# Pooled q and k in four buffers each, v of batch 0 pooled by two additions, the exponent table loaded at the start, no forced filler matmuls, and a new order for every engine

## The chip, the core and the metric

The kernel runs on one core of a Trainium2 chip, as one program on its engines: TensorE (PE in the rows; PEld is its weight load), VectorE (DVE), ScalarE (ACT), GpSimd (POOL) and SyncE (SP, which only issues transfers here). The metric is the device time of one launch in microseconds; lower is better.

## The reference

Three stages in a chain. The inputs of the last two are set so that every product of the matrices is wanted at nearly float32 precision, which the kernel reaches by splitting each operand into a high and a low float32r part and adding three matmuls.

```python
# attention: B, H, S, D = 4, 8, 576, 64; pooled by 4 along S, plus a local band of +-3
q_d, k_d, v_d = (mean over groups of 4 positions of q, k, v)      # 144 positions
out_d     = softmax(q_d k_d^T / sqrt(D)) v_d
out_local = softmax(q k^T / sqrt(D), only |i - j| < 4) v
x = (repeat(out_d, 4) + out_local) as (2304, 512)
# first stage: 2304 x 512 -> 2048 -> 512
h = relu(x w_in); x = (s * h * h + b) w_out
# second stage: 2304 x 512 -> 1536 -> 512
return ((x w_a) * (x w_b)) w_out
```

## The kernel before, in words

**Stages.** The first stage of the MLP runs in 6 blocks of 384 positions; each block is 16 iterations of 12 matmuls into `h` and 12 into four `acc` banks (`a_iter`, L1044), 24 matmuls of 384 columns per iteration, 2304 in all. Its input for block i, `xsh` and `xsl`, comes from the attention. The second stage (`b_group`, matmuls at L1347 and L1487 to L1489) follows when the last block is done.

**Attention on two engines.** Batch 0 and the first 192 positions of batch 1 are done as 8 *tiles* of 96 positions on TensorE (`tile_job`): scores, maximum (DVE), exponents (ACT), division (DVE), transposes (PE), copies (ACT), product with v (PE), sum with the pooled part (DVE), split into `xsh` (ACT) and `xsl` (DVE). Most later positions are done as 13 *units* on VectorE (`unit`, "the band" below): products `pr`, sums, exponents, products with v, three additions of which the last, at L984, writes the unit's output `o`; then four transposes on PE, `bt` at L999, put it in the layout that the first stage needs. The pooled attention of a batch and a pair of heads is `down`: sums over four positions (`kd`, `qd` from DVE for batch 0, from POOL for the others), scores, maximum `nb`, exponents, transposes, copies, product with pooled v. For batches 1 to 3 the pooled v, `pv`, is summed by accumulating transfers that POOL issues (`pool_in`, L551); for batch 0 DVE sums it by a reduction over a strided view (L603).

**Weights.** The weights come as 64-bit words. Each of the 32 slices of the first stage needs three ACT instructions (L342, L349, L378) and three DVE instructions (L354, L362, L383) before PE can use it. The exponents of the tiles, the copies and these slices all stand in ACT's one queue. The stretch from the start until the last slice is done is called the ramp here. When the ramp's work is over, its buffers are given to the band (`open_b`), so the first `pr` of the band comes after the last slice.

**What sets the order.** `Program` collects tasks with an engine, a planned duration, what they read and the buffers they take; `Program.order` simulates the engines with the planned durations and writes each engine's instructions in the order in which its simulation starts them. Each engine then runs its own list strictly in that order. A few instructions are put in by the function of another engine's task and have no duration in the plan: the two casts of the mask and of the identity on DVE (`i_fn`, `m_fn`, L293 to L301), which stand in DVE's list wherever the plan happens to issue the two transfers on SP. PE's idle time ahead of the first `h` is filled with matmuls on zeros (`keep_warm`, `pw` at L273): 18 at the start, then in front of each PE task at least `FILL_MIN` of them.

Of the kernel before, what the change touches and what calls it, by code (L numbers as in the profile page):

```python
# [55 lines left out]
MAX_STAGED = 4  # L56

# [52 lines left out]
class Program:  # L110
# [26 lines left out]
    def order(self):  # L137
# [9 lines left out]
        clock, warming = Clock(), True  # L147
# [10 lines left out]
        while len(out) < len(self.tasks):  # L158
# [47 lines left out]
            at[t.eng] = t.end  # L206
            avail[t.eng].remove(t)
# [26 lines left out]
def moe_chain(ctx, tc, qT, kT, vd, tq, tk, tv, qu, ku, vu, w_a1, w_o1, w_a2, w_b2, w_o2, sb, ident_d, bmask_d, emask_d, out):  # L234
# [19 lines left out]
    ones = const.tile([128, 2], F32, name="ones")  # L254
    bc = const.tile([128, HP], F32, name="bc")
# [283 lines left out]
    def pool_in(b, after, due):  # L539
# [3 lines left out]
        for r in range(4):  # L543
            for kh in range(2):
                def fn(p, r=r, kh=kh):
# [8 lines left out]
                    "POOL" if r else "SP", 1.25, fn, (), [("pv", b)] if r == 3 else (), () if r + kh else [("pv",)], (), due,  # L554
                    [t[kh]] if r else [t[0]] if kh else after, seen=6.0,
                )

    def down(b, hp, ph, pool_eng, v_eng, due=1e9):
# [16 lines left out]
        for name, src in (("k", "dk"), ("q", "dq")):  # L575
            eng = pool_eng[name == "q"]

            def prep(p, name=name, eng=eng):
# [9 lines left out]
                eng, dve(S) if eng == "DVE" else 1.25, prep, [(src, key)], [(name + "d", key)],  # L588
                [(ph + name + "d",)], [ph + (dq if src == "dq" else src)] if b else (),
            )  # L590
        if b == 0:
            for kh in range(2):
                def lv(p, kh=kh):
                    st["v", kh] = new(ph, "dv", [HK, 4, 2 * D])
                    return st["v", kh], vd[b, hp, :, kh]

                load(lv, HK * 2048, writes=[("dv", key, kh)], acq=[(ph + "dv",)], after=after)

                def vprep(p, kh=kh):
                    x = st["v", kh]  # L600
                    d = st["vp", kh] = new(ph, "vp", [HK, 2 * D])
                    if v_eng == "DVE":
                        V.tensor_reduce(out=d, in_=x.rearrange("p r c -> p c r"), axis=AX.X, op=ALU.add)  # L603
                    else:
                        G.tensor_tensor(out=x[:, 0:2], in0=x[:, 0:2], in1=x[:, 2:4], op=ALU.add)
                        G.tensor_tensor(out=d, in0=x[:, 0], in1=x[:, 1], op=ALU.add)

                add(
                    v_eng, dve(512) if v_eng == "DVE" else 1.1, vprep, [("dv", key, kh)], [("vp", key, kh)],
                    [(ph + "vp",)], [ph + "dv"],  # L610
                )
# [75 lines left out]
        def o_fn(p):  # L687
# [9 lines left out]
            "PE", 0.6, o_fn, [("aT", key), ("upslot", b)] + ([("vp", key, 0), ("vp", key, 1)] if b == 0 else [("pv", b)]),  # L697
            [("o", key)], [wide], [pick(ts, 2)] + ([ph + "vp", ph + "vp"] if b == 0 else ["pv"] if hp == HP - 1 else []),
# [992 lines left out]
```

## Time and profile before

| | |
|---|---|
| device time, median of 3 runs | 936.18 us (935.21 to 938.07) |
| span of the profiled execution, first to last instruction | 932.3 us |
| so outside the span, against the three runs | 2.9 to 5.8 us, 3.9 at the median |
| PE busy | 913.2 us, 98% of the span |
| DVE busy | 789.9 us, 85% |
| ACT busy | 497.4 us, 53% |
| POOL busy | 69.7 us, 7% |
| mean granted TensorE clock | 0.994 of full speed |

The profile gives the span of its execution and no device time of that execution; sums below are made on the span and then moved by the 3.9 us to the median. The shares are means over stages that differ: ACT is busy nearly all the time in the first 140 us and little afterwards.

### The profile page before, as it was taken

What the parts mean: (1) busy time and instruction counts of PE and PEld (TensorE: products, weight loads), DVE (VectorE), ACT (ScalarE), POOL (GpSimd) and SP (SyncE); (2) the same over time, 40 slices, a digit from 0 to 9 for tenths busy, and PEclk for the clock granted to TensorE, in tenths of its full rate; (3) what the DMA queues carried; (4) which work ended last, traced back from release to release, by engine and by line L of the source; (5) the groups of instructions that cost most, each with busy time, mean ns of one, the idle gap of its engine ahead of it and who ended that gap; (6) DMA issues with size and microseconds to landing.
All of it is one profiled execution on the core that took longest, in us unless ns stands there. A gap on an engine that the chain in (4) does not pass through costs nothing.

```text
span 932.3 us, 14367 instructions
## 1 busy us (share of the span) xinstructions
PE 913.2 (98%) x5319; PEld 847.0 (91%) x5319; DVE 789.9 (85%) x1388; ACT 497.4 (53%) x1144; POOL 69.7 (7%) x70
## 2 busy tenths in 40 slices
PE   8988999999999999999999999999999999999997
PEld 4667989998999899999999999999999999999996
DVE  6988998999999999995977999879877778877753
ACT  4989995345445443535988555335433336433322
POOL 2241201021322200000000000000000000000000
PEclk9998999999999999999999999999999999999999
DMA  7869626224354332313477342012200010300001
GB/s 206 241 174 332 156 90 194 82 82 133 115 115 114 103 107 69 102 29 136 148 262 261 122 122 82 23 44 81 102 22 3 24 43 13 102 29 18 1 1 69
DMA packets 46864, 96.76 MB, mean 104 GB/s; under 512 B 6393, under 2 KB 21337, under 8 KB 46409
## 3 DMA queue, kind: packets, MB, share of 16 engines
q1 hardware_dynamic: 39160, 92.77, 31.0%
q0 software_dynamic: 7200, 2.67, 2.5%
q8 instruction: 42, 0.69, 0.3%
q10 hardware_dynamic: 432, 0.39, 0.1%
q14 instruction: 30, 0.24, 0.1%
HBM read 83.22 MB, written 12.58 MB: 103 GB/s over the span
## 4 chain that ended last, share of the span: by engine, by line
PE 84%; DVE 5%; ACT 4%; issue 3%; DMA 2%; POOL 1%; SPq 0%; ACTq 0%
PE ab L1347 28%; PE acc L1102 7%; PE acc L1103 6%; PE h L1059 6%; PE acc L1104 6%; PE h L1061 6%; PE h L1060 6%; PE acc L1488 5%; PE acc L1489 5%; PE acc L1487 5%; DVE pr L969 1%; DMA pv<-in_vd_dram 1%; ACT z L342 1%; DMA tq<-in_bmask_dram 1%; ACT w L378 1%
## 5 line engine op out<-in xcount | busy, mean ns | idle before, releaser
L1347 PE MATMUL ab<-xo,w 128*128 128x384 f32 x1376 | 273.7, 338 | 0.4 <-DVE u L1390 0.4
L1347 PEld LDWEIGHTS ab<-xo,w 128*128 128x128 f32 x1376 | 246.1, 188 | 16.3 <-DVE u L1390 0.7
L1102 PE MATMUL acc<-gh,w 128*128 128x384 f32 (+1 forms) x384 | 134.2, 350 | 4.0 <-ACT w L816 2.0
L1103 PE MATMUL acc<-gl,w 128*128 128x384 f32 x384 | 131.2, 342 | 0.0
L1059 PE MATMUL h<-xsh,w 128*128 128x384 f32 x384 | 131.1, 341 | 0.0
L1104 PE MATMUL acc<-gh,w 128*128 128x384 f32 (+1 forms) x384 | 130.5, 340 | 0.0
L1061 PE MATMUL h<-xsh,w 128*128 128x384 f32 x384 | 129.0, 336 | 0.0
L1060 PE MATMUL h<-xsl,w 128*128 128x384 f32 x384 | 129.0, 336 | 0.0
L1076 ACT ACTIVATE u<-h 128x384 f32<-128x384 f32 x96 | 47.1, 491 | 116.3 <-PE h L1061 114.9
L1463 ACT ACTIVATE gh<-u 128x384 fp32r<-128x384 f32 x69 | 36.2, 524 | 84.6 <-DVE u L1424 50.5
L1102 PEld LDWEIGHTS acc<-gh,w 128*128 128x128 f32 x384 | 73.0, 190 | 8.1 <-ACT w L816 2.6
L1059 PEld LDWEIGHTS h<-xsh,w 128*128 128x128 f32 x384 | 72.2, 188 | 2.4 <-issue 2.0
L1103 PEld LDWEIGHTS acc<-gl,w 128*128 128x128 f32 x384 | 73.1, 190 | 0.9 <-DVE gl L1087 0.9
L1104 PEld LDWEIGHTS acc<-gh,w 128*128 128x128 f32 x384 | 73.0, 190 | 0.0
L1060 PEld LDWEIGHTS h<-xsl,w 128*128 128x128 f32 x384 | 72.2, 188 | 0.0
L1061 PEld LDWEIGHTS h<-xsh,w 128*128 128x128 f32 x384 | 72.1, 188 | 0.0
L1087 DVE TENSOR_TENSOR gl<-u,gh 128x384 fp32r<-128x384 f32 x96 | 54.3, 565 | 15.4 <-ACT gh L1083 15.2
L1371 ACT ACTIVATE w<-ab 128x384 f32<-128x384 f32 x31 | 15.2, 491 | 95.2 <-PE ab L1347 93.4
L1489 PE MATMUL acc<-w,gl 128*128 128x512 f32 x138 | 54.4, 394 | 0.0
L1488 PE MATMUL acc<-w,gh 128*128 128x512 f32 x138 | 54.3, 394 | 0.0
L1487 PE MATMUL acc<-w,gh 128*128 128x512 f32 x138 | 54.2, 393 | 0.0
L354 DVE TENSOR_SCALAR w<-w 128x512 uint16<-128x512 f32 x61 | 45.6, 767 | 8.3 <-ACT w L349 8.0
(207 smaller groups left out, 1743.9 us busy)
## 6 DMA issues: line engine op xcount, KB each, us to landing
w<-in_w_a_dram SPq DMA_DIRECT2D x26, 512.0 KB
w<-in_w_o_dram SPq DMA_DIRECT2D x25, 512.0 KB
bk<-in_ku_dram SPq DMA_DIRECT2D x22, 320.0 KB
bk<-in_vu_dram SPq DMA_DIRECT2D x22, 320.0 KB
w<-wod SPq DMA_DIRECT2D x12, 512.0 KB
w<-in_w_b_dram SPq DMA_DIRECT2D x10, 512.0 KB
x2d<-ev SPq DMA_DIRECT2D x24, 192.0 KB
x<-x2d SPq DMA_DIRECT2D x3, 1536.0 KB
```

Of the source, the lines that this page charges most:

```text
L1059: nc.tensor.matmul(out=st["h"], lhsT=w[:, 0, k], rhs=hi[:, k], start=(k == 0), stop=False)
L1060: nc.tensor.matmul(out=st["h"], lhsT=w[:, 0, k], rhs=lo[:, k], start=False, stop=False)
L1061: nc.tensor.matmul(out=st["h"], lhsT=w[:, 1, k], rhs=hi[:, k], start=False, stop=(k == HP - 1))
L1076: A_.activation(out=st["u"], in_=st["h"], func=ACTF.Relu)
L1087: V.tensor_tensor(out=st["lo"], in0=st["u"], in1=st["hi"][:, :n].bitcast(F32), op=ALU.subtract)
L1102: nc.tensor.matmul(out=acc, lhsT=wh, rhs=st["hi"], start=(f == 0), stop=False)
L1103: nc.tensor.matmul(out=acc[:, :n], lhsT=wh, rhs=st["lo"], start=False, stop=False)
L1104: nc.tensor.matmul(out=acc, lhsT=wl, rhs=st["hi"], start=False, stop=(f == FA - 1))
L1347: nc.tensor.matmul(out=o, lhsT=w[:, k], rhs=x, start=(not more and k + n == 0), stop=(k == 1 and n == 2), skip_group_check=more,)
L1487: nc.tensor.matmul(out=acc, lhsT=gh, rhs=w[:, 0], start=first, stop=False)
L1488: nc.tensor.matmul(out=acc, lhsT=gh, rhs=w[:, 1], start=False, stop=False)
L1489: nc.tensor.matmul(out=acc, lhsT=gl, rhs=w[:, 0], start=False, stop=last)
```

## The change

- `RAMP_BUFS`: four buffers each for `qd` and `kd` in the ramp where there was one; the buffers `dv` and `vp` are gone.
- v of batch 0 is loaded by one transfer of 72 x 1024 elements per pair of heads into a weight buffer `w`, and summed in place by two additions (72 x 512, then 72 x 256 elements) where there were two transfers and two reductions.
- An exponent of two columns, `warm`, stands first in ACT's list, so that the table load is at the start.
- `FILL_MIN` is 0: filler matmuls stand only where the plan has idle time. There are 81 of them, 87 before.
- Numbers of the plan: matmuls of the first stage 1/2185 us a column (1/2220 before), of the second 0.1762 us (0.173) and 0.2315 us (0.231); POOL's pooling 2.3 us (1.25), its transfers seen after 5.0 us (6.0); SP's transfers are planned with an issue time and a shared rate.
- The order of all engines is planned anew with these numbers.

```diff
-WARM, FILL_MIN, FILL_MAX = 18, 1, 20
-RAMP_BUFS = {"dq": 2, "dk": 2, "dv": 2, "qd": 1, "kd": 1, "vp": 4, "tq": 1, "tk": 1, "tv": 2, "e": 1, "x": 1, "z": 2}
+WARM, FILL_MIN, FILL_MAX = 18, 0, 20
+RAMP_BUFS = {"dq": 2, "dk": 2, "qd": 4, "kd": 4, "tq": 1, "tk": 1, "tv": 2, "e": 1, "x": 1, "z": 2}
...
+            if t.bytes:
+                wire = max(wire, s + DMA_START) + t.bytes / DMA_RATE
+                t.end = max(t.end, wire + DMA_LAND)
...
         keep_warm(WARM)
         V.memset(ones, 1.0)
+        A_.activation(out=warm, in_=ones, func=ACTF.Exp)
...
-                    if v_eng == "DVE":
-                        V.tensor_reduce(out=d, in_=x.rearrange("p r c -> p c r"), axis=AX.X, op=ALU.add)
...
+            def vprep(p):
+                x = st["v"]
+                V.tensor_tensor(out=x[:, :, 0:2], in0=x[:, :, 0:2], in1=x[:, :, 2:4], op=ALU.add)
+                V.tensor_tensor(out=x[:, :, 0], in0=x[:, :, 0], in1=x[:, :, 1], op=ALU.add)
...
-        per = n / 2220
+        per = n / 2185
...
-                    "PE", 6 * 0.173, fn, [("xo", t, i), (GREAD[PRODUCTS[i]],) + key], [("p", key, i)],
+                    "PE", 6 * 0.1762, fn, [("xo", t, i), (GREAD[PRODUCTS[i]],) + key], [("p", key, i)],
```

**First place: the start of DVE's list**, the pooling of q and k of batch 0 (`kd`, `qd`) and the first maxima (`nb`). Before:

```order
L582 TENSOR_REDUCE kd_124<-w_112 128x144
L582 TENSOR_REDUCE qd_128<-w_120 128x144
L582 TENSOR_REDUCE kd_143<-w_122 128x144
L582 TENSOR_REDUCE qd_147<-w_126 128x144
L634 TENSOR_REDUCE nb_149<-sc_135 72x2
L634 TENSOR_REDUCE nb_149<-sc_136 72x2
L301 CAST bmaskb_77<-tq_167 96x306
L296 CAST identb_76<-ident_75 96x96
L637 TENSOR_SCALAR nb_149<-nb_149 72x4
```

And now:

```order
L309 CAST bmaskb_77<-tq_114 96x306
L590 TENSOR_REDUCE kd_137<-w_123 128x144
L590 TENSOR_REDUCE qd_141<-w_125 128x144
L304 CAST identb_76<-ident_75 96x96
L590 TENSOR_REDUCE kd_147<-w_127 128x144
L590 TENSOR_REDUCE qd_153<-w_129 128x144
L590 TENSOR_REDUCE kd_157<-w_131 128x144
L590 TENSOR_REDUCE qd_169<-w_133 128x144
L590 TENSOR_REDUCE kd_175<-w_135 128x144
L634 TENSOR_REDUCE nb_185<-sc_163 72x2
L634 TENSOR_REDUCE nb_185<-sc_164 72x2
L590 TENSOR_REDUCE qd_198<-w_139 128x144
```

The reductions of all four pairs of heads now stand ahead of the row that ends the first maximum (`L637 TENSOR_SCALAR nb`, the next row), and the cast of the identity stands behind the first pair. On SP the mask is now the first transfer, and the identity the tenth, behind the mask and the eight loads of q and k; before, the mask was the ninth and the identity the tenth.

**Second place: POOL's list for batch 1**, its pooling of q and k (`dk` to `kd`, `dq` to `qd`, two instructions each) among its accumulating transfers (`pv`). Before:

```order
L551 DMA pv_181<-in_vd_dram 72x4x128
L584 ISA
L584 TENSOR_TENSOR dk_241<-dk_241 128x144x2
L585 TENSOR_TENSOR kd_319<-dk_241 128x144
L584 TENSOR_TENSOR dq_259<-dq_259 128x144x2
L585 TENSOR_TENSOR qd_348<-dq_259 128x144
L551 DMA pv_181<-in_vd_dram 72x4x128 x4
L584 TENSOR_TENSOR dk_343<-dk_343 128x144x2
```

And now:

```order
L592 TENSOR_TENSOR dq_183<-dq_183 128x144x2
L593 TENSOR_TENSOR qd_313<-dq_183 128x144
L592 TENSOR_TENSOR dk_188<-dk_188 128x144x2
L593 TENSOR_TENSOR kd_347<-dk_188 128x144
L592 TENSOR_TENSOR dq_196<-dq_196 128x144x2
L593 TENSOR_TENSOR qd_402<-dq_196 128x144
L559 DMA pv_171<-in_vd_dram 72x4x128
L592 TENSOR_TENSOR dk_328<-dk_328 128x144x2
```

The second pair of heads is now pooled ahead of the second accumulating transfer; before, four of those transfers stood in front of it.

**Third place: PE's list at the last transpose of the band** (`bt`), in the fifth block of the first stage. Before:

```order
L1059 MATMUL h_4944<-xsh_3492,w_1744 128x384
L1060 MATMUL h_4944<-xsl_3493,w_1744 128x384
L1061 MATMUL h_4944<-xsh_3492,w_1744 128x384
L999 MATMUL bt_4955<-ident_75,o_4877 128x128 x4
L1102 MATMUL acc_4516<-gh_4905,w_1688 128x384
```

And now:

```order
L1102 MATMUL acc_4471<-gh_4856,w_1582 128x384
L1103 MATMUL acc_4471<-gl_4873,w_1582 128x384
L1104 MATMUL acc_4471<-gh_4856,w_1582 128x384
L999 MATMUL bt_4893<-ident_75,o_4808 128x128 x4
L1059 MATMUL h_4899<-xsh_3480,w_1648 128x384
```

Counted from the first `h`, 1836 matmuls of the first stage stood ahead of this transpose before, and 1806 now. At the 13 transposes the counts were 504, 624, 744, 936, 978, 1092, 1236, 1284, 1398, 1470, 1596, 1716 and 1836; now they are 486, 606, 726, 942, 954, 1074, 1194, 1266, 1398, 1440, 1566, 1686 and 1806. On DVE the instructions ahead of the last unit's `o` are the same in number and kind, but for one `gl` less (L1087, one per iteration of the first stage) and the pooling of v.

## Rows read from the trace of the kernel before

**Rows 1.** Busy time by stretch: us, engines' busy (instructions), granted clock, DMA share, GB/s.

```profile
70.00:80.00 10.00, 7.42 (x50) 5.56 (x46) 8.73 (x19) 10.00 (x33) 1.21 (x1) 0.93 0.89 283
80.00:90.00 10.00, 9.98 (x57) 9.62 (x58) 8.42 (x16) 8.87 (x29) 1.19 (x1) 0.73 1.06 380
11.00:142.00 131.00, 119.46 (x919) 98.79 (x918) 119.20 (x247) 121.64 (x382) 30.02 (x28) 0.96 0.67 192
146.00:426.00 280.00, 279.58 (x1698) 269.92 (x1697) 268.47 (x388) 129.51 (x312) 39.49 (x38) 1.00 0.36 102
430.00:500.00 70.00, 70.00 (x402) 69.82 (x401) 52.00 (x85) 56.64 (x108) 0.00 (x0) 1.00 0.63 215
```

**Rows 2.** ACT's waits, 11 to 143 us: times in all, count, longest.

```profile
ACT w L683 <- PE at L671: 3.2, 1, 3.2
ACT w L647 <- DVE nb L637: 2.6, 3, 1.8
ACT u L1076 <- PE h L1061: 1.1, 1, 1.1
ACT e L816 <- DVE tnb L805: 0.6, 1, 0.6
...
ACT w L683 <- DVE tsm L824: 0.3, 1, 0.3
```

**Rows 3.** DVE and PE around the first and the last transpose, in order of time.

```profile
168.26 0.42 DVE L984 TENSOR_TENSOR o<-pr 128x256 f32<-128x256 f32 x1
168.88 0.60 PE L999 MATMUL bt<-ident,o 128*128 128x128 f32 x4
...
424.88 0.43 DVE L984 TENSOR_TENSOR o<-pr 128x256 f32<-128x256 f32 x1
426.44 0.60 PE L999 MATMUL bt<-ident,o 128*128 128x128 f32 x4
```

**Rows 4.** DVE at the start, in order of time.

```profile
3.58 0.75 DVE L582 TENSOR_REDUCE kd<-w 128x144 f32<-128x576 f32 x1 [2.49 <-DMA w<-in_kT_dram]
...
8.14 0.75 DVE L582 TENSOR_REDUCE kd<-w 128x144 f32<-128x576 f32 x1 [3.10 <-PE sc L620]
...
10.55 0.32 DVE L301 CAST bmaskb<-tq 96x306 bf16<-96x306 f32 x1 [0.27 <-DMA tq<-in_bmask_dram]
...
11.00 0.16 DVE L637 TENSOR_SCALAR nb<-nb 72x4 f32<-72x4 f32 x1
...
11.73 0.74 DVE L582 TENSOR_REDUCE qd<-w 128x144 f32<-128x576 f32 x1
12.39 0.81 DVE L634 TENSOR_REDUCE nb<-sc 72x2 f32<-72x288 f32 x2
```

**Rows 5.** SP's issues of the mask and of the identity.

```profile
4.66 0.51 SPq L300 DMA_DIRECT2D tq<-in_bmask_dram  x1
5.22 0.47 SPq L295 DMA_DIRECT2D ident<-in_ident_dram  x1
```

**Rows 6.** ACT's table load, its first exponent, and the ramp's last weight copy.

```profile
11.24 1.28 ACT L647 ACT_TABLE_LOAD   x1 [11.24 <-DVE nb L637]
12.53 0.38 ACT L647 ACTIVATE e<-sc,nb 72x144 f32<-72x144 f32 x1
...
141.64 0.63 ACT L378 ACTIVATE w<-z 128x512 fp32r<-128x512 f32 x1
```

**Rows 7.** DVE's last weight row and the band's first product.

```profile
142.31 0.69 DVE L383 TENSOR_TENSOR w<-z,w 128x512 fp32r<-128x512 f32 x1
...
146.44 2.02 DVE L908 TENSOR_TENSOR pr<-bq,bk 128x1792 f32<-128x1792 f32 x1 [0.28 <-DMA bq<-in_qu_dram]
```

**Rows 8.** POOL's second pair of heads, and PE waiting for the next.

```profile
42.88 1.15 POOL L584 TENSOR_TENSOR dk<-dk 128x288 f32<-128x288 f32 x1
...
54.69 1.24 PE L620 MATMUL sc<-kd,qd 64*72 64x144 f32 x8 [2.55 <-POOL qd L585]
```

**Rows 9.** DVE's reductions of v, two in one row, and an addition of 512.

```profile
32.52 1.99 DVE L603 TENSOR_REDUCE vp<-dv 72x128 f32<-72x512 f32 x2
...
51.02 0.68 DVE L383 TENSOR_TENSOR w<-z,w 128x512 fp32r<-128x512 f32 x1
```

More of the change, by code (lines that the diff above doesn't have):

```diff
@@ L56 @@
 MAX_STAGED = 4
+POOL_LAND, POOL_PREP = 5.0, 2.3
 T_ENG, S_ENG, X2_ENG = "D", "DD", "DDDDDDD"
@@ L84 @@
         "eng", "dur", "fn", "deps", "succ", "acq", "picks", "rel", "due", "lead", "share", "num", "left", "ready", "start",
-        "end", "fill", "seen",
+        "end", "fill", "seen", "bytes",
     )
@@ L146, in order @@
         at = {e: 0.0 for e in ENGINES}
-        clock, warming = Clock(), True
+        clock, warming, wire = Clock(), True, 0.0
         at["PE"] = clock.run(1.07, 0.17 * WARM, 1.0)
@@ L553, in pool_in, with down @@
                 t[kh] = add(
-                    "POOL" if r else "SP", 1.25, fn, (), [("pv", b)] if r == 3 else (), () if r + kh else [("pv",)], (), due,
-                    [t[kh]] if r else [t[0]] if kh else after, seen=6.0,
+                    "POOL" if r else "SP", 1.25 if r else 0.46, fn, (), [("pv", b)] if r == 3 else (), () if r + kh else [("pv",)], (), due,
+                    [t[kh]] if r else [t[0]] if kh else after, seen=POOL_LAND if r else 0.0, nbytes=460e3 if r else 200e3,
                 )
-    def down(b, hp, ph, pool_eng, v_eng, due=1e9):
+    def down(b, hp, ph, pool_eng, due=1e9):
         st = {}
@@ L591, in down, with lv @@
         if b == 0:
[L592 to L601, printed above, removed]
-                    if v_eng == "DVE":
-                        V.tensor_reduce(out=d, in_=x.rearrange("p r c -> p c r"), axis=AX.X, op=ALU.add)
[L604 to L611, printed above, removed]
+            def lv(p):
+                st["v"] = slot(p[0], F32).rearrange("p a m -> p (a m)").rearrange("p (k r d) -> p k r d", k=2, r=4)[:HK]
+                return st["v"], vd[b, hp]
+            tv0 = load(lv, HK * 4096, writes=[("dvl", key)], acq=[("w",)], after=after)
+            def vprep(p):
+                x = st["v"]
+                V.tensor_tensor(out=x[:, :, 0:2], in0=x[:, :, 0:2], in1=x[:, :, 2:4], op=ALU.add)
+                V.tensor_tensor(out=x[:, :, 0], in0=x[:, :, 0], in1=x[:, :, 1], op=ALU.add)
+            add("DVE", dve(512) + dve(256), vprep, [("dvl", key)], [("dv", key)])
         def vpool(kh):
-            return st["vp", kh] if b == 0 else pooled[b][:, kh, hp]
+            return st["v"][:, kh, 0] if b == 0 else pooled[b][:, kh, hp]
         def s_fn(p):
@@ L1544, in moe_chain @@
     for hp in range(HP):
-        down(0, hp, "r", DOWN_ENG[hp], "DVE", target(0) - DUE_DOWN[0] + DUE_DOWN[1] * hp)
+        down(0, hp, "r", DOWN_ENG[hp], target(0) - DUE_DOWN[0] + DUE_DOWN[1] * hp)
     for i in first:
@@ L1551, in moe_chain @@
     for hp in range(HP):
-        down(1, hp, "r", ("POOL", "POOL"), "POOL", target(FA) - DUE_NEXT[0] + DUE_NEXT[1] * hp)
+        down(1, hp, "r", ("POOL", "POOL"), target(FA) - DUE_NEXT[0] + DUE_NEXT[1] * hp)
     for i in ramp[len(first):]:
@@ L1569, in moe_chain @@
             for hp in range(HP):
-                down(downs, hp, "b", ("POOL", "POOL"), "POOL", due - DUE_DOWN[2] + DUE_DOWN[3] * hp)
+                down(downs, hp, "b", ("POOL", "POOL"), due - DUE_DOWN[2] + DUE_DOWN[3] * hp)
             downs += 1
```

15 lines of the change are left out of this document (9 added, 6 removed).

## The prediction

> **What bounds the kernel now.** I read the busy time by stretch first. From 11 to 142 us ACT is busy 121.64 of 131 us; from 146 to 426 us PE is busy 279.58 of 280 and DVE 268.47 of 280; from 430 us on PE alone is full, 402 matmuls in 70.00 us, 0.174 us each [rows 1]. So there are three stages with three limits: a ramp that ACT's queue sets, a band in which PE and DVE are both full, and a rest that only PE sets. A change in the ramp is worth what it moves the start of the band; a change in the band is worth what it does to the balance between PE and DVE.
>
> Then I read ACT's waits. Between its first exponent, at 12.53 us, and the end of the last weight copy, at 142.27, lie 129.7 us [rows 6]. Eight groups of waits lie in them: those shown, and three of 0.4 us left out, 9.0 us together [rows 2]. The other 120.7 us are work, one instruction behind the other.
>
> Last I looked at where PE takes over from DVE in the band. The first unit's output is written until 168.68 and the transposes start at 168.88; the last is written until 425.31 and transposed at 426.44 [rows 3]. PE comes 0.2 to 1.1 us after the data exist: neither waits for the other, but neither has room.
>
> **The change part by part.**
>
> *The start of DVE.* Before, DVE did two pairs of heads by the time the mask landed, waiting 3.1 us for the one `kd` buffer in between; the mask was the ninth transfer and landed at about 10.5 us [rows 4, 5]. With four buffers that wait goes. But the cast of the identity now stands behind the first pair, and the identity is the tenth transfer, behind the same nine. So I put its cast at 10.6 us, and DVE waits there with one pair done. From there the order has five reductions of 0.66 us (11.73 to 12.39), the first maximum at 0.8, one more reduction, and then the row that frees ACT: 10.8 + 3.3 + 0.8 + 0.7 = 15.6 us. ACT started 0.24 us after that row began (11.00 to 11.24) [rows 4, 6], so its first exponent comes at 15.8 us, 3.3 us later than before.
>
> *The table load* took 1.28 us in front of the first exponent [rows 6]. Moved to the start it lies under the wait for DVE, which lasts until 15.8 us either way, so it is worth nothing in the sum; if that cover were gone it would be worth the 1.28 us.
>
> The Trainium skill (ScalarE: Activation LUTs, section What ACT_TABLE_LOAD costs) gives about 1.28 us for the load and 1.38 us more for a drain, 2.66 us for a switch. Here the exponent starts 1.29 us after the load, so the trace shows the first part and no second. By the page the credit could be 2.66 us, and the sum would be the same, since the wait for DVE covers both.
>
> *ACT's queue up to the last weight copy* holds the same instructions as before, but for two short ones. So its end is 15.8 + 120.7 us and its waits. The longest wait, 3.2 us, came about because POOL had the second pair of heads of batch 1 behind four accumulating transfers, done only from 42.88 us, and PE waited 2.55 us for the third [rows 8]; now the second pair stands ahead of those transfers, and no single buffer ties POOL to PE. The second longest, 2.6 us for `nb`, came from the same single buffers at batch 0. I take both as gone and the rest as it was: 3.2 us of waits, so the last copy ends at 139.7 us, 2.6 us sooner. The bounds are no waits at all, 5.8 us sooner, and as many as before, 3.2 us later. New waits are possible where the planned order meets a late landing: the first instructions on weight slices now stand among the copies of batch 0's transposed exponents (L683), for which PE waits; that is what the later bound is for.
>
> *Pooling of v.* Eight reductions at 1.0 us become four pairs of additions, of 512 elements at 0.68 us [rows 9] and of 256 at 0.43, the band's last addition having that size [rows 3]: 8.0 us less 4.4, 3.6 us off DVE. DVE has 119.20 us of 131 in the ramp and ACT has more [rows 1], so ACT's queue hides it and I count nothing; were DVE the limit of the ramp it would be the whole 3.6 us.
>
> *Filler matmuls.* Six fewer, and none forced between the tiles. PE waits for ACT and DVE there, so nothing, unless the clock falls (below).
>
> *The band* begins when DVE has finished the last slice, 143.00 us, and a load has come, 146.44 [rows 7]. Both follow ACT's last copy, so I move the band 2.6 us forward as a whole. Ahead of the last unit's output DVE's list is otherwise the same, but for one `gl` less; an addition of 512 took 0.68 and this one is of 384, so 0.4 to 0.7 us, and I take 0.4. So the last output exists at 425.31 - 2.6 - 0.4 = 422.3 us.
>
> *The place of the transposes on PE.* The new plan holds PE slower by 1.6%, and so puts the last transpose behind 1806 matmuls, not 1836. That is 30 x 0.174 = 5.2 us of PE's work that moves from ahead of this transpose to behind it. PE would come to it at 426.44 - 5.2 = 421.2 us, or sooner by what it gains in the ramp. DVE isn't there before 422.3, so PE waits; what PE gained in the ramp is given back in this wait. With 0.2 us from output to transpose as at the first unit, it starts at 422.5, 3.9 us earlier than before, with 5.2 us more behind it. Nothing but PE's work follows, so the end moves by 5.2 - 3.9 = +1.3 us.
>
> *The second stage* has other weight buffers and a few moved groups. PE was full in it, so I count nothing.
>
> **The sum** is 932.3 + 1.3 = 933.6 us of span. Outside the span lie 3.9 us at the median of the runs: 937.5 us. With the two bounds on ACT's waits the last transpose moves from 7.1 us earlier (5.8 + 0.4 + 0.9, the last being the 1.1 us after the output less 0.2) to 1.9 us later (3.2 - 0.4 - 0.9), and the time goes from 934.3 to 943.3 us.
>
> **Rivals.**
>
> 1. *The ramp gives more, and DVE is ready when PE comes: faster.* ACT's waits vanish wholly and DVE's 3.6 us shorten the chain ahead of its first exponents, too. For it: the order takes up both long waits, and v's reductions stood among the first exponents' rows. Against it: the identity's cast, and that ACT starts later. With 5.8 us from the waits, 2 of the 3.6 us, the 0.4 for the `gl` and the 0.9 us by which PE came later than it had to, the last transpose comes 9.1 us earlier, and the time is 936.2 + 5.2 - 9.1 = 932.3 us. It decides from a last transpose 8.0 us earlier on: then the time is more than 2.8 us below the 936.2.
>
> 2. *The clock falls when PE waits: slower.* In the band PE is now to wait some microseconds at transposes where it waited 0.4 us in all. After the stretch from 70 to 80 us, in which PE was busy 7.42 of 10 us, the granted clock of the next 10 us was 0.73, part of it at the lower of the two levels, 1.2 GHz, which costs 2.7 us of full-speed work; from 146 to 426 us it was 1.00 [rows 1]. In front of a transpose that waits for DVE such a loss eats only PE's wait; at the last one it is paid. Then 937.5 + 2.7 = 940.2 us. It decides if a fall comes at the last transpose or behind it.
>
>    The Trainium skill (TensorE: Matmul & The Clock Gate, section Why this matters for your kernels) warns that idle gaps between bursts of matmuls put the array back to the lower clock. The stretches at 70 and 80 us agree with it, and by it this rival would be the rule and not the exception.
>
> 3. *The ramp comes later.* ACT has new waits for weights or for POOL in place of the old, 9.0 us as before, and its later start stays: the band begins 3.2 us later. PE's 5.2 us are then paid in full: 943 us.
>
> 4. *Nothing is gained or lost.* DVE's last output comes as much earlier as PE's place in its list: the last transpose 4.9 to 5.2 us earlier, and the time 936.2 to 936.5 us.
>
> **How the numbers follow.** Likeliest 0.52, 937.5 us, its own range 935.5 to 940; rival 1 0.15; rival 2 0.15; rival 3 0.10; rival 4 0.08. The predicted time is that of the first. A difference under about 0.3%, 2.8 us, can't be told from no change here. Faster by more is rival 1, 0.15. Slower by more, above 939.0 us, are rivals 2 and 3 and 0.06 of the first, 0.31. The rest, 0.54, is within. The range leaves out half of rival 1 below and most of rival 3 above: 933.2 to 941.5 us.
>
> **What would show it.** Right: DVE idle until about 10.6 us ahead of the identity's cast; ACT's first exponent at 15 to 16.5 us; the ramp's last weight copy (now at L386) at 138 to 141 us; PE waiting for DVE's `o` at `bt`, some microseconds together, where it waited 0.2; the last transpose at 421 to 424 us. Wrong: if the first exponent comes before 13 us, the identity landed early and the first term falls; if ACT's waits up to the last copy are over 6 us, the order of the ramp has not done what I credit it with; if PE doesn't wait at `bt`, DVE's list got shorter by something that I don't see, and the kernel is faster; if the granted clock falls between 146 and 430 us, it is rival 2.

## The result and the profile after

The changed kernel takes 944.76 us at the median (943.14 to 945.17, 4 runs), before 935.69 beside it: ratio 1.0102, interval 1.0054 to 1.015. The profiled execution took 945.17 us with a span of 943.4. The forecast was 937.5 us with a range of 933.2 to 941.5; that the kernel would be slower by more than 2.8 us had a chance of 0.31, and it is slower by 9.1. Of all executions below one, of e14, took 1483.67 us at a mean granted clock of 0.556 of full speed; the ratios and the spreads leave it out.

The busy time by stretch of the kernel after, with the columns of [rows 1]:

```profile
17.00:144.00 127.00, 116.22 (x912) 97.82 (x911) 113.55 (x243) 119.59 (x381) 25.55 (x28) 0.96 0.65 188
146.00:426.00 280.00, 276.67 (x1680) 266.30 (x1679) 269.11 (x387) 126.91 (x309) 44.36 (x38) 1.00 0.37 103
430.00:500.00 70.00, 69.00 (x392) 68.09 (x391) 49.94 (x83) 55.12 (x104) 0.00 (x0) 1.00 0.60 207
500.00:530.00 30.00, 28.14 (x155) 26.51 (x154) 24.92 (x41) 23.34 (x44) 0.00 (x0) 1.00 0.70 255
```

PE does 18 matmuls fewer than in [rows 1] in the same 280 us of the band, and 10 fewer in the 70 us from 430 on, where it had been full. The second loss is one that the prediction did not count.

ACT in order of time, to be read against [rows 6]:

```profile
0.75 1.28 ACT L300 ACT_TABLE_LOAD   x1 [0.75 <-PEq L1671]
2.04 0.20 ACT L300 ACTIVATE warm<-ones 128x2 f32<-128x2 f32 x1
17.37 0.38 ACT L647 ACTIVATE e<-sc,nb 72x144 f32<-72x144 f32 x1 [15.13 <-DVE nb L637]
...
142.89 0.62 ACT L386 ACTIVATE w<-z 128x512 fp32r<-128x512 f32 x1
```

DVE in order of time, against [rows 4], [rows 7] and [rows 3]:

```profile
2.95 0.32 DVE L309 CAST bmaskb<-tq 96x306 bf16<-96x306 f32 x1 [1.86 <-DMA tq<-in_bmask_dram]
...
12.30 0.20 DVE L304 CAST identb<-ident 96x96 bf16<-96x96 f32 x1 [6.32 <-DMA ident<-in_ident_dram]
...
17.12 0.15 DVE L637 TENSOR_SCALAR nb<-nb 72x4 f32<-72x4 f32 x1
...
143.55 0.69 DVE L391 TENSOR_TENSOR w<-z,w 128x512 fp32r<-128x512 f32 x1 [1.00 <-ACT w L386]
...
147.65 2.03 DVE L908 TENSOR_TENSOR pr<-bq,bk 128x1792 f32<-128x1792 f32 x1 [2.50 <-DMA bq<-in_qu_dram]
...
425.61 0.43 DVE L984 TENSOR_TENSOR o<-pr 128x256 f32<-128x256 f32 x1
```

The identity's cast waits 6.32 us, until 12.30. ACT's first exponent is 4.84 us later than before, its last copy ends at 143.51 against 142.27, and the band starts 1.2 us later.

ACT's waits from 17 to 144 us, as in [rows 2] (the first is the start):

```profile
ACT e L647 <- DVE nb L637: 15.1, 1, 15.1
ACT e L816 <- DVE tsm L827: 2.3, 1, 2.3
ACT w L816 <- DVE sm L655: 1.8, 1, 1.8
ACT w L647 <- DVE sm L658: 0.9, 1, 0.9
ACT u L1076 <- PE h L1061: 0.8, 1, 0.8
```

The two waits of [rows 2] that were to vanish are gone, and others, of 2.3, 1.8 and 0.9 us, stand in their place. All three are for DVE, whose work in the ramp the prediction had held to be hidden behind ACT's.

PE at the seventh, the eighth and the last transpose and at the start of the second stage, in order of time:

```profile
308.74 0.66 PE L999 MATMUL bt<-ident,o 128*128 128x128 f32 x4 [1.20 <-DVE o L984]
...
325.19 0.41 PE L999 MATMUL bt<-ident,o 128*128 128x128 f32 x2 [0.95 <-DVE o L984]
...
427.30 0.60 PE L999 MATMUL bt<-ident,o 128*128 128x128 f32 x4
...
520.42 3.32 PE L1347 MATMUL ab<-xo,w 128*128 128x384 f32 x18
524.40 2.65 PE L1347 MATMUL ab<-xo,w 128*128 128x384 f32 x12 [0.65 <-DVE w L1411]
528.15 0.62 PE L1347 MATMUL ab<-xo,w 128*128 128x384 f32 x2 [1.11 <-DVE w L1411]
```

PE's waits, first from 146 to 428.5 us (one row), then from 480 to 560:

```profile
PE bt L999 <- DVE o L984: 2.2, 2, 1.2
...
PE ab L1347 <- DVE w L1411: 1.8, 2, 1.1
PE acc L1102 <- ACT gh L1083: 0.8, 1, 0.8
```

The first row is the wait that the prediction named, but not at the place that it named: both parts of it, 1.20 and 0.95 us, lie in the middle of the band. PE came to the last transpose straight from matmuls, without a wait, 1.26 us after the output was there. The last two rows were not in the prediction; in the same window before, there is one wait of 0.4 us:

```profile
PE ab L1347 <- DVE u L1390: 0.4, 1, 0.4
```

Behind most of PE's waits stands ACT. Its waits for transfers from 425 to 530 us were 1.9 us before:

```profile
ACT w L342 <- DMA w<-in_w_b_dram: 0.7, 1, 0.7
ACT w L349 <- DMA w<-in_w_a_dram: 0.6, 1, 0.6
ACT w L349 <- DMA w<-in_w_b_dram: 0.6, 1, 0.6
```

They are 9.9 us after, of which these rows are 9.3:

```profile
ACT wx L357 <- DMA wx<-in_w_a_dram: 3.2, 2, 2.0
ACT w L357 <- DMA w<-in_w_b_dram: 2.6, 3, 1.4
ACT ev L1129 <- DMA x2d<-ev: 2.4, 1, 2.4
...
ACT w L357 <- DMA w<-in_w_a_dram: 1.1, 1, 1.1
```

ACT prepares the second stage's weights there, and its queue holds conversions whose transfers haven't landed; `gh` of the first stage stands behind them. Two of PE's waits, followed back through the engines in order of time:

```profile
494.01 0.68 ACT L357 ACTIVATE w<-w 128x512 int32<-128x512 uint16 x1 [0.43 <-DMA w<-in_w_b_dram]
494.58 0.51 ACT L1083 ACTIVATE gh<-u 128x384 fp32r<-128x384 f32 x1
495.14 0.44 PE L1102 MATMUL acc<-gh,w 128*128 128x384 f32 x1 [0.80 <-ACT gh L1083]
...
523.52 1.23 ACT L1129 ACTIVATE ev<-acc,bc,sbt 128x384 f32<-128x384 f32 x2 [2.38 <-DMA x2d<-ev]
524.65 1.06 ACT L1289 ACTIVATE w<-w 128x1024 fp32r<-128x1024 f32 x1
525.74 1.23 DVE L1293 TENSOR_TENSOR w<-w 128x1024 fp32r<-128x1024 f32 x1
527.55 0.55 DVE L1411 TENSOR_TENSOR w<-w,ab 128x384 f32<-128x384 f32 x1
```

The second chain ends in the wait of 1.11 us above. It does not start at a weight: ACT waits 2.38 us for the buffer of `ev`, which a transfer is still writing out to `x2d`, and the split of a weight (L1289, L1293) comes behind it. Ahead of PE's wait of 0.65 us, DVE itself waited 0.56 us for a transfer, `x`.

### The profile page after: what moved, and what is told of

The parts are those of the page before. It is cut to its first block, busy times and chain, and to the rows that moved or that the text cites. A ratio compares the mean times of both kernels' runs of the same rounds, so it can differ in the third digit from the quotient of the medians.

```text
span 943.4 us, 14338 instructions
## 1 busy us (share of the span) xinstructions
PE 912.3 (97%) x5313; PEld 845.6 (90%) x5313; DVE 789.0 (84%) x1388; ACT 496.4 (53%) x1145; POOL 70.1 (7%) x70
## 4 chain that ended last, share of the span: by engine, by line
PE 74%; DVE 9%; ACT 8%; DMA 6%; issue 3%; SPq 0%; ACTq 0%; DVEq 0%
PE ab L1347 28%; PE acc L1488 5%; PE acc L1489 5%; PE acc L1487 5%; PE h L1059 5%; PE h L1060 5%; PE h L1061 5%; PE acc L1103 4%; PE acc L1102 4%; PE acc L1104 4%; DMA tv<-in_tv_dram 2%; DVE pr L969 2%; DVE gl L1087 1%; ACT w L357 1%; DVE pr L908 1%
## 5 line engine op out<-in xcount | busy, mean ns | idle before, releaser
L1347 PE MATMUL ab<-xo,w 128*128 128x384 f32 x1366 | 276.4, 338 | 1.8 <-DVE w L1411 1.8
L1347 PEld LDWEIGHTS ab<-xo,w 128*128 128x128 f32 x1366 | 243.9, 188 | 19.6 <-DVE w L1411 2.4
L1102 PE MATMUL acc<-gh,w 128*128 128x384 f32 (+1 forms) x384 | 131.5, 343 | 2.3 <-ACT e L816 1.3
L1059 PE MATMUL h<-xsh,w 128*128 128x384 f32 x384 | 132.0, 344 | 0.5 <-ACT w L386 0.5
L1104 PE MATMUL acc<-gh,w 128*128 128x384 f32 (+1 forms) x384 | 129.5, 337 | 0.0
L1061 PE MATMUL h<-xsh,w 128*128 128x384 f32 x384 | 129.1, 336 | 0.2 <-DVE w L391 0.2
L1463 ACT ACTIVATE gh<-u 128x384 fp32r<-128x384 f32 x68 | 35.7, 524 | 89.2 <-DVE u L1424 49.0
L1102 PEld LDWEIGHTS acc<-gh,w 128*128 128x128 f32 x384 | 72.1, 188 | 5.7 <-ACT e L816 1.9
L1059 PEld LDWEIGHTS h<-xsh,w 128*128 128x128 f32 x384 | 72.1, 188 | 2.6 <-issue 1.8
L1061 PEld LDWEIGHTS h<-xsh,w 128*128 128x128 f32 x384 | 72.1, 188 | 0.5 <-DVE w L391 0.5
L1104 PEld LDWEIGHTS acc<-gh,w 128*128 128x128 f32 x384 | 72.2, 188 | 0.0
L1371 ACT ACTIVATE w<-ab 128x384 f32<-128x384 f32 x33 | 16.2, 491 | 99.0 <-PE ab L1347 93.2
L1087 DVE TENSOR_TENSOR gl<-u,gh 128x384 fp32r<-128x384 f32 x96 | 55.0, 573 | 8.2 <-ACT gh L1083 8.2
L1080 ACT ACTIVATE u<-u 128x384 f32<-128x384 f32 x96 | 50.8, 529 | 1.9
L1083 ACT ACTIVATE gh<-u 128x384 fp32r<-128x384 f32 x96 | 50.6, 527 | 1.8
L908 DVE TENSOR_TENSOR pr<-bq,bk 128x1792 f32<-128x1792 f32 (+1 forms) x26 | 48.9, 1880 | 2.8 <-DMA bq<-in_qu_dram 2.5
L1489 PE MATMUL acc<-wx,gl 128*128 128x512 f32 x129 | 50.8, 394 | 0.0
```

The source lines that it names most:

```text
L908: V.tensor_tensor(out=pr, in0=st["q", h].unsqueeze(2).to_broadcast([128, R, 7, D]), in1=window(st["k", h], R), op=ALU.mult,)
L1059: nc.tensor.matmul(out=st["h"], lhsT=w[:, 0, k], rhs=hi[:, k], start=(k == 0), stop=False)
L1061: nc.tensor.matmul(out=st["h"], lhsT=w[:, 1, k], rhs=hi[:, k], start=False, stop=(k == HP - 1))
L1080: A_.activation(out=st["u"], in_=st["u"], func=ACTF.Square)
L1083: A_.activation(out=st["hi"][:, :n], in_=st["u"], func=ACTF.Copy)
L1087: V.tensor_tensor(out=st["lo"], in0=st["u"], in1=st["hi"][:, :n].bitcast(F32), op=ALU.subtract)
```

## The experiments

Two theories stood at the start. **O**: the new numbers in the plan cost the time, through the order that follows from them. **P**: a changed part itself costs it (the v loads, the buffers, the early table load, the missing fillers). A plan is made anew by every change of a number, so the kernels are compared place by place. In the table, "start" is ACT's first exponent; "w80" how many of the first stage's 32 weight loads SP has issued by 80 us; "copy" the end of the last weight copy; then the time at which PE starts the 486th and the 1806th main matmul (L1059 to L1061, L1102 to L1104, L1347, L1487 to L1489, counted in each trace); "loss" what the 300 matmuls from the 2100th to the 2400th, between the stages, take above the 53.4 us of before; "wait" ACT's waits for transfers from 425 to 530 us, summed. Times in us.

| kernel | median | start | w80 | copy | 486th | 1806th | loss | wait |
|---|---|---|---|---|---|---|---|---|
| before | 935.7 | 12.5 | 20 | 142.3 | 165.6 | 421.0 | 0 | 1.9 |
| after | 944.8 | 17.4 | 15 | 143.5 | 168.6 | 427.1 | 4.4 | 9.9 |
| e1 code, old numbers | 931.0 | 11.1 | 21 | 137.6 | 161.2 | 417.1 | 0 | 0.9 |
| e2 before, new numbers | 953.0 | 16.5 | 11 | 147.4 | 174.2 | 432.2 | 5.3 | 11.9 |
| e3 identity early | 945.8 | 12.4 | 19 | 140.4 | 165.4 | 423.8 | 8.6 | 10.6 |
| e4 old price, stage 1 | 943.9 | 15.6 | 18 | 141.8 | 166.1 | 421.4 | 4.4 | 13.5 |
| e5 e1, new loads | 945.9 | 16.2 | 16 | 141.0 | 167.6 | 425.2 | 2.7 | 12.5 |
| e6 e1, new prices | 935.9 | 11.6 | 17 | 146.0 | 169.7 | 428.2 | 0.6 | 2.9 |
| e7 e1, no forced fillers | 935.1 | 11.7 | 18 | 142.7 | 166.0 | 421.5 | 0 | 0.9 |
| e8 e1, new POOL numbers | 936.2 | 12.3 | 14 | 150.0 | 173.6 | 429.2 | 0 | 1.7 |
| e9 after, old loads | 933.7 | 11.5 | 20 | 138.7 | 161.9 | 420.3 | 0.6 | 2.9 |
| e10 after, fillers | 947.1 | 16.2 | 19 | 140.6 | 165.9 | 424.9 | 5.4 | 13.1 |
| e11 before, four buffers | 935.8 | 13.0 | 20 | 140.4 | 164.6 | 424.1 | 0 | 1.6 |
| e12 before, v and table | 933.7 | 11.3 | 22 | 138.0 | 161.2 | 416.4 | 0 | 1.8 |
| e13 after, slow landing | 964.1 | 15.7 | 17 | 156.9 | 180.3 | 451.9 | 0.3 | 0 |
| e14 e1, one buffer | 942.1 | 11.8 | 8 | 148.3 | 174.8 | 429.8 | 0 | 0.7 |
| e15 e1, identity early | 929.8 | 11.2 | 22 | 136.6 | 160.2 | 416.2 | 0 | 1.4 |
| e16 after, six `tv` | 950.8 | 16.8 | 10 | 147.7 | 171.6 | 428.8 | 10.0 | 10.3 |
| e17 e15, six `tv` | 936.2 | 12.5 | 18 | 145.2 | 168.3 | 423.8 | 0.2 | 1.1 |

A median covers 4 to 10 executions and the other columns one of them; executions of one kernel spread by up to 11 us (below), so the two don't always agree. The execution in the other columns was the shortest of its kernel in e4 (939.27 us), e5 (941.80) and e12 (929.40), the longest in e8 (941.67) and the longest but one in e6 (942.35).

**Code and numbers apart.** e1 puts the old numbers back into the changed kernel; e2 puts the new ones into the kernel before. Left out of the cut are the loads and transfers of `pv`, POOL's pooling and the second stage's prices.

```diff
-WARM, FILL_MIN, FILL_MAX = 18, 0, 20
+WARM, FILL_MIN, FILL_MAX = 18, 1, 20
-        return add("SP", 0.46, fn, reads, writes, acq, rel, due, after, seen=0.0, nbytes=nbytes)
+        return add("SP", max(0.45, nbytes / 235e3), fn, reads, writes, acq, rel, due, after)
-        per = n / 2185
+        per = n / 2220
...
```

> The changed kernel's code (four buffers, one v load and two additions, table load first) with all the old numbers in the plan (matmul prices, load costs, POOL costs, forced fillers). Theory O (the order that the new numbers give costs the time): within 2 us of before, 934 to 938 us. Rival P (the changed parts themselves cost the time): near the changed kernel, 942 to 946 us.

> The kernel before with all the new numbers in its plan and none of the changed parts. Theory O: near the changed kernel, 942 to 946 us. Rival P: within 2 us of before, 934 to 938 us.

e1: 930.99 us, ratio to before 0.9949 (0.9929 to 0.9969). e2: 953.00, ratio 1.0184 (1.0152 to 1.0217). P falls: with the old numbers the changed code gains about 5 us, and the new numbers cost 14 us on the one code and 17 on the other, more than O had expected.

The 5 us go with the granted clock. Each execution's mean clock is on record: at 0.998 the kernel before took 931.58 us beside e1, and e1 929.89 to 932.04; at 0.994 before took 933.53 and e1 932.84 and 934.47. But e1's ten lie at 0.994 to 0.999, and most of before's at 0.987 to 0.993. So most of the gain comes with a higher clock under the new order; at one clock the two kernels lie within about 2 us of each other. The loss of the changed kernel does not go that way: at 0.989 to 0.991 it took 943.1 to 945.2 us, and before, over all its executions, 934.2 to 939.7.

**One cause at a time in the changed kernel.** e3 moves one transfer and nothing else; e4 changes one price.

```diff
-        nc.sync.dma_start(out=ident, in_=ident_d)
         V.tensor_copy(out=identb, in_=ident[:TQ, :TQ])
...
         nc.sync.dma_start(out=bm, in_=bmask_d)
+        nc.sync.dma_start(out=ident, in_=ident_d)
```

> The changed kernel with the identity's transfer issued right behind the mask's; the cast keeps its place and nothing else moves. If the 6.3 us for which VectorE waits at the identity's cast set the end: ScalarE's first exponent at 11 to 13 us instead of 17.4, the first `pr` of the band 3 to 5 us sooner and 939 to 941 us. If the loads of weights set the end of the ramp instead: the exponent moves as much, but the first `pr` less than 1 us, and 943.5 to 945 us.

> The changed kernel with the old price of a first-stage matmul (n/2220 for n/2185) in its plan, and nothing else changed. If the new price places the band's transposes and the second stage's first weights too early for what comes before them: PE's delay against the kernel before stays near 3 us at matmul 486, stays below 4 at 1806 and below 5 at 2400, and 938 to 940 us. If the price has nothing to do with it: 943 to 946 us, with 6 us at 1806 and 10 at 2400 as in the changed kernel.

e3: 945.84 us, ratio 1.0093 (1.0063 to 1.0123). The wait is gone; DVE's cast in its trace, in order of time:

```profile
6.44 0.20 DVE L303 CAST identb<-ident 96x96 bf16<-96x96 f32 x1
```

The exponent came 5.0 us sooner, the first `pr` 3.2 us sooner (144.50), the last transposes 3.3 us sooner, and the end not at all: 8.6 us were lost between the stages where 4.4 had been. Of these 4.2 us more, about 3.4 are the granted clock, which fell to its lower level, 1.2 GHz, at 494.5 and at 528.7 us, for 3.4 us each time (0.17, 0.07 and 0.10 of the three stretches of 10 us shown at point 6 below). So the identity did hold the ramp, and the ramp was not what the end hung on; neither expectation holds whole, as the first `pr` came sooner and the end did not. e4: 943.88 us, 1.0086 (1.0056 to 1.0116). The band kept step with before: from the 486th to the 1806th matmul 255.3 us, before 255.4 and the changed kernel 258.5. No kernel with the new price did; e6, which below has the new prices alone, takes 258.5 where e1 takes 255.9. The loss between the stages stayed at 4.4. So the price is the band's 3 us and not the rest. What that is worth at the end is open: the traced execution of e4 ended 6.0 us sooner than that of the changed kernel, but it was the shortest of seven, and the median is 0.9 us sooner.

**The numbers one by one on e1.** e5 to e7 each turn one of the edits above round again (e5 with the first loads of `pv`, e6 with the second stage's prices); e8 makes this one and its like for the transfers of `pv`.

```diff
-                eng, dve(S) if eng == "DVE" else 1.25, prep, [(src, key)], [(name + "d", key)],
+                eng, dve(S) if eng == "DVE" else POOL_PREP, prep, [(src, key)], [(name + "d", key)],
```

> The code of the changed kernel with the old numbers, and of the new ones only those of the loads (0.46 us to issue, then 380 kB per us and 1 us to land, where the old number made a load hold SP's place for its bytes at 235 kB per us and land 2 us later). Theory L (the plan believes in loads that are faster than they are, issues few and late and puts their users early): 940 to 946 us, with PE's delay against e1_code_oldnumbers growing both in the ramp and between matmul 2100 and 2400. Rival (the loads' numbers cost nothing by themselves): 930 to 933 us.

> As e1_code_oldnumbers, with the new matmul prices (n/2185, 0.1762, 0.2315) alone. By theory L the prices cost at most what they gave back in e4_price_stage1, where the last transpose came 5 to 6 us sooner but the end 1 us: 931 to 935 us. Rival (prices set where the band's transposes and second-stage weights stand, and that costs the end): 936 to 941 us.

> As e1_code_oldnumbers, with no forced filler matmul (FILL_MIN 0). If the forced fillers keep the granted clock at its upper level where it falls without them: the ramp loses 1 to 4 us, 932 to 935 us. Rival (they only take PE's time): 930 to 931.5 us.

> As e1_code_oldnumbers, with the new numbers of GpSimd alone (2.3 us for pooling q or k, 5 us for an adding transfer to land and its 460 kB on the wire). They bear on batches 1 to 3 only, whose work the plan then starts later or sooner by a few us: 930 to 933 us. Rival (batch 1's operands come too late for its tiles, and ScalarE and VectorE stand still ahead of the band): 934 to 938 us.

e5: 945.92, 1.0088 (1.0056 to 1.0121). e6: 935.91, 1.0007 (0.9977 to 1.0036). e7: 935.06, 0.9983 (0.9961 to 1.0005). e8: 936.24, 0.9982 (0.9952 to 1.0013). The loads' numbers alone bring all of the 14 us. By the medians each of the others takes 4 to 5 us from e1 and leaves the kernel where before was; by the ratios it is 3 to 5.5 us, and the intervals of e7 and e8 overlap that of e1. These costs don't add up, as e9 shows, which has all three of them, and in part they are the clock again: at 0.996 e8 took 930.83 to 933.04 us, and e1 at 0.995 to 0.997 931.50 and 931.97. The loads are another matter: at 0.989 to 0.993 e5 took 941.8 to 946.9, and before beside it 933.1 to 939.0.

**The loads' numbers taken out, and fillers put in.** e9 makes the diff's second edit above in the changed kernel, and its like for the first loads of `pv`. e10 leaves the plan alone:

```diff
-            keep_warm(t.fill)
+            warm_up = warm_up and "acc" not in t.rel
+            keep_warm(max(t.fill, 1) if warm_up and t.eng == "PE" else t.fill)
```

> The changed kernel with the old numbers for its loads alone; new matmul prices, GpSimd numbers and no forced fillers stay. By theory L, and with the 4 to 5 us that each of the other new numbers took alone in e6 to e8: 934 to 940 us, with no more than 2 us lost between matmul 2100 and 2400. Rival (the new numbers together cost as much without the loads' one): 941 to 946 us.

> The changed kernel's plan as it is, and in the program at least one filler matmul ahead of each of TensorE's pieces of work until the first main matmul. If the half-rate stretches of the changed kernel (11.1 to 17.9 and 31.6 to 41.8 us) set its ramp: they shrink or go, and the first `pr` of the band comes 2 to 4 us sooner, 940 to 943 us. Rival (SyncE's queue and the weights behind it set the ramp): less than 1 us at the first `pr`, 943.5 to 946 us.

e9: 933.68 us, 0.9984 (0.9958 to 1.0009), 11 us under the changed kernel, with 0.6 us lost between the stages and 2.9 us of ACT's waits for transfers. That and e5 show from both sides that the loads' numbers cost the time. e10: 947.08, 1.0138 (1.0084 to 1.0192). The stretch at the lower clock from 31.6 to 41.8 us is gone from its trace, that at 11 us is not and 3.4 us at 86 us are new; the first `pr` came 2.8 us sooner (144.82), and again nothing arrived at the end; neither expectation holds whole.

**The parts one by one.** e11 sets `"qd": 4, "kd": 4` in the kernel before. e12 leaves its plan alone, puts the early exponent in and replaces each reduction of v:

```diff
-                        V.tensor_reduce(out=d, in_=x.rearrange("p r c -> p c r"), axis=AX.X, op=ALU.add)
+                        V.tensor_tensor(out=x[:, 0:2], in0=x[:, 0:2], in1=x[:, 2:4], op=ALU.add)
+                        V.tensor_tensor(out=d, in0=x[:, 0], in1=x[:, 1], op=ALU.add)
```

> The kernel before with four buffers each for pooled q and k, its plan made anew with the old numbers, nothing else changed. If the four buffers bring the 5 us that e1_code_oldnumbers is ahead of before: 930 to 932 us, and as many weights issued by 80 us as there (21, before 20). Rival (the v loads and additions or the table load bring it): 935 to 937 us.

> The kernel before with its plan as it is, v of batch 0 summed by two additions (in the place of each of the eight reductions) and the table load first. If these bring the 5 us: 930 to 932 us. Rival (hidden, as the prediction had it): 934 to 937 us, the first exponent 1.3 us sooner at most.

e11: 935.84, 1.0007 (0.9983 to 1.0032). e12: 933.73, 0.9975 (0.9949 to 1.0002), some 2 us that can't be told from none.

**What in the loads' numbers, and what is left.** e13 changes one line of the changed kernel, e14 takes e1 with `"qd": 1, "kd": 1`, e15 takes e1 with e3's edit.

```diff
-DMA_START, DMA_RATE, DMA_LAND = 1.0, 380e3, 1.0
+DMA_START, DMA_RATE, DMA_LAND = 1.0, 235e3, 2.0
```

> The changed kernel with a load still 0.46 us in SyncE's queue, but its bytes on the wire at 235 kB per us and 2 us to land, in the plan. If the plan's belief in early landings costs the time: 934 to 940 us as in e9_after_oldloads, and ScalarE waits less than 4 us for transfers between 425 and 530 us (9.9 in the changed kernel). If the short seat in SyncE's queue costs it (many loads issued ahead, and weights stuck behind loads that wait for a buffer): 942 to 946 us.

> As e1_code_oldnumbers with one buffer each for pooled q and k instead of four. If the v load in one piece (four loads instead of eight, none of which waits for a buffer) brings the gain: 930 to 933 us. If the four buffers do, together with it: 934 to 937 us.

> As e1_code_oldnumbers with the identity's transfer issued right behind the mask's; nothing else moves. If its landing holds VectorE up there too: 1 to 3 us sooner, 928 to 930 us. Rival (hidden in this order): 930 to 932 us.

e13: 964.13, 1.0309 (1.0273 to 1.0345), outside both expectations. It holds an answer all the same: with late landings in the plan ACT waits for no transfer between the stages and nothing is lost there, while the ramp is 12 us and the band 13 us longer than in the changed kernel. That fits the belief in early landings as what makes the loss between the stages, with something else in the new model behind the ramp. It is not shown: PE comes to the 1806th matmul 25 us later there, and the same transfers would then be in time without any change of order. e14: 942.05, 1.0068 (1.0047 to 1.009): without the four buffers the code loses 11 us, twice what it had gained, outside both expectations. Alone they bring nothing (e11); whether they are needed for themselves or the plan without them happens to be poor can't be told. e15: 929.76, 0.9952 (0.9926 to 0.9978), the lowest median of the study, 1 us from e1; its ratio to before is that of e1 (0.9949), so a gain over e1 isn't shown.

What else stands in the ramp showed in SP's queue. SP's issues in the changed kernel, in order of time:

```profile
33.91 0.33 SPq L285 DMA_DIRECT2D w<-in_w_a_dram  x1
34.33 0.38 SPq L285 DMA_DIRECT2D dq<-in_qT_dram  x1
42.98 18.49 SPq L285 DMA_DIRECT2D tv<-in_tv_dram  x5
61.52 0.35 SPq L285 DMA_DIRECT2D w<-in_w_o_dram  x1
```

And in e1:

```profile
37.66 0.44 SPq L285 DMA_DIRECT2D w<-in_w_a_dram  x1
...
47.87 9.58 SPq L285 DMA_DIRECT2D tv<-in_tv_dram  x4
57.50 0.35 SPq L285 DMA_DIRECT2D w<-in_w_o_dram  x1
```

No weight is issued for 27.6 us in the one and for 19.8 in the other, and the loads ahead of it are `tv`, which wait for a buffer. So e16 and e17 gave `tv` six buffers.

```diff
-"tq": 1, "tk": 1, "tv": 2, "e": 1
+"tq": 1, "tk": 1, "tv": 6, "e": 1
```

> The changed kernel with six buffers for the tiles' `tv` in the ramp instead of two, its plan made anew. If the weights stand behind `tv` loads that wait for a buffer: no stretch of 27 us without a weight's issue, 19 or more weights issued by 80 us (15), matmul 486 at 161 to 166 us (168.6) and 936 to 942 us, what is lost between the stages staying. Rival (the buffers of weights, which ScalarE and VectorE free in the order of the plan, hold them back): 15 to 17 weights and 943 to 946 us.

> As e15_oldnumbers_identity with six `tv` buffers in the ramp. If the waits of SyncE for `tv` buffers (20.4 us between 20 and 90 us in e1_code_oldnumbers) still hold weights back there: 924 to 928 us. Rival (ScalarE, full from 60 to 140 us, sets the ramp): 929 to 931 us.

e16: 950.78, 1.0146 (1.0125 to 1.0167). e17: 936.15, 1.0001 (0.9984 to 1.0017). Both are worse than the kernels that they start from, and outside what was expected: this theory fell. SP then stands still for other buffers; its longest waits from 20 to 90 us are, in e16,

```profile
SPq L285 <- PE sc L780: 18.2, 1, 18.2
```

and in e17

```profile
SPq L285 <- PE sc L780: 11.1, 1, 11.1
```

What holds in most of the table is that few weights issued by 80 us go with a late 486th matmul (8 to 17: 168 to 180 us; 18 to 22: 160 to 168). The granted clock goes with it as closely. The stretches at the lower clock between 5 and 100 us add up to 0 to 7 us in e1, e7, e9, e12 and e15 (486th at 160 to 166 us), to 10 in before, e5, e10, e11 and e17 (165 to 168) and to 17 to 24 in the other nine (165 to 180). The plan's order alone doesn't set the count of weights either: e10 has the order of the changed kernel, 7 us less at the lower clock, and issues 19 weights by 80 us instead of 15. That the three go together is shown; which of them comes first is open.

## Why the prediction was wrong

The sum can be laid beside the trace term by term, and closes: 933.6 + 3.8 + 1.0 + 5.0 = 943.4 us of span. (The time outside the span, 3.9 us in the sum, was wrong as well: it set the span of one execution against the median of others. Of one and the same execution it is 1.7 to 2.4 us in all of e1 to e17, and 1.8 in the profiled one of the changed kernel. So the time missed by 7.3 us and the span by 9.8.)

1. *ACT's queue*, the first step that failed: 139.7 us was forecast for the last copy and 143.5 measured, 3.8 us later. The form was right: start, work and waits. The start was 17.4 and not 15.8 us, because the identity, issued at 5.13 us, was there only at 12.3 and not at 10.6; e3 shows what that was worth in the ramp. The work was 119.1 us (120.7 forecast). The waits were 7.0 us and not 3.2, and that is the term that failed: those that I struck out went, and new ones for DVE came, as the later bound (9.0) allowed. e1, with the code's order from the old numbers, has 6.7 us of waits and starts at 11.1.
2. *The table load*: hidden here, as forecast. In e1 the first exponent is at 11.1 us, where the table load began before. The load took 1.28 us and the next instruction of ACT started 0.01 us after its end. The 1.38 us of drain in the Trainium skill (ScalarE: Activation LUTs, section What ACT_TABLE_LOAD costs) don't show in any run here; the load is ACT's first instruction in all of them, so no run shows a switch behind other work.
3. *The band on DVE*: right. The last `o` was forecast for 422.3 us and ended at 426.04, later by 3.7, which is the ramp's 3.8.
4. *The transposes*: right that the new places make PE wait, wrong at the last one. PE waits 2.2 us at `bt`, but at the seventh and the eighth. At the last, "DVE isn't there before 422.3, so PE waits" did not happen: PE, 3.0 us late from the ramp at the 486th matmul and 6.1 us late at the 1806th, came without a wait 1.3 us after the output and not 0.2, which is the 1.0; DVE waited for it. e4 and e6 show that the price does the band's part: with the old one PE loses nothing in the band against before. Of the other kernels with the old price only e11 (4 us) and e5 (2 us) lose there, too, and for e11 I have no cause.
5. *The second stage*, "I count nothing", the step that failed worst: 516.1 us lie behind the last transpose, where 505.9 of before and the 5.2 moved there were forecast, so 5.0 us. PE being full there before said that nothing was late, not how much room there was, and the new plan moved the preparation of its weights. The table parts the kernels cleanly: with the new loads' model at 380 kB per us ACT waits 9.9 to 13.5 us for transfers and 2.7 to 10.0 us are lost; without it at most 2.9 us and 0.6. PE's waits shown above are 2.8 of the changed kernel's 4.4 us.
6. *The rivals.* Rival 3 had the time (943 us) and half of the mechanism: ACT's late start was there, but it made the band 1.2 us late and not 3.2, and the end between the stages was not in it. Rival 2 looked for a fall of the clock in the band; the falls were in the ramp, and taking one away (e10) changed nothing at the end. In e3 the clock did fall where PE waits between the stages:

```profile
490.00:500.00 10.00, 8.19 (x36) 7.62 (x36) 7.99 (x13) 8.21 (x17) 0.00 (x0) 0.83 0.78 283
...
520.00:530.00 10.00, 7.04 (x33) 5.95 (x32) 7.91 (x14) 4.70 (x8) 0.00 (x0) 0.93 0.48 167
530.00:540.00 10.00, 10.00 (x49) 9.43 (x49) 9.33 (x17) 3.21 (x6) 0.00 (x0) 0.90 0.01 2
```

   The Trainium skill (TensorE: Matmul & The Clock Gate, section Why this matters for your kernels) has it that gaps between bursts of matmuls bring the lower clock. e3 agrees: ahead of its two falls PE had waited 1.66 us (until 492.70) and 2.96 us (until 527.89). In the changed kernel, with waits of 0.65 and 1.11 us in the same place, the clock stayed at 1.00 from 500 to 530 us.

The parts of the change, which took most of the prediction's length, were a gain of 5 us together, most of it with the clock, and the numbers, which I read only for what they did to the transposes, were the change. What stays open: how the new loads' model lengthens the ramp, which of late weights and lower clock comes first there, and how much of what the plan's other numbers cost on e1 is more than the clock.

## What to carry to other kernels

Where a planner sets the order, a corrected number is a change to every queue and can cost more than the code beside it gains: put the old numbers under the new code and the new under the old before looking for causes. A plan that believes transfers to land early puts the work on them early into queues that run in order, and whatever stands behind it there waits too; look for the waits for transfers of the engine that prepares data, in each stage, the full ones too. A gain at the start counts only if nothing downstream takes it back: two kernels here lost 3 us of it between the band and the second stage, one of them with a falling clock. Look at the granted clock of every execution before a few us are put down to an edit.

## What the runs showed of the hardware

The identity is 64 KB and was issued 0.62 us after the last of eight transfers of 288 KB; DVE could use it 7.2 us after its issue. Issued second (e3), it was there by 6.44 us, 5.3 us after its issue at most.

Executions of one kernel, with nothing changed, spread by up to 10.8 us: e8 took 930.83 us at the least and 941.67 at the most. The profiled one took longest, and its granted clock was at the lower level from 54.8 to 58.2 and from 68.5 to 82.1 us; the row of the second stretch:

```profile
60.00:80.00 20.00, 17.17 (x117) 12.26 (x114) 12.78 (x27) 12.95 (x36) 0.85 (x1) 0.71 0.58 183
```

In e1, whose ten executions lie within 5.5 us, the same stretch has

```profile
60.00:80.00 20.00, 18.09 (x145) 15.21 (x143) 18.45 (x39) 20.00 (x60) 1.19 (x1) 1.00 0.91 307
```

and no stretch at the lower level between 5 and 926 us. The mean clocks of e8's executions agree: 0.996 in the four that took 930.83 to 933.04 us, 0.993 in those of 936.03 to 937.32, 0.990 in that of 941.67. In the kernel before, on one chip, they go from 0.998 (931.20 us) to 0.985 (941.31). That time and clock go together is shown; only one execution of each kernel was traced, so what lowers the clock in one and not in the next isn't.
